# Four more tiles transposed by DMA, and a new order around them, in the opening of an FNet and MLP kernel

## The chip, the cores and the metric

The kernel runs on one core of one Trainium2 chip. The metric is the device time of one execution in microseconds (us), the median over runs of the same program. Besides the runs that are only timed there is one profiled execution, whose trace gives all durations below.

## The reference

The input is x of 2048 rows and 576 columns. It is normalized by row, and two branches are added to it: the real part of a Fourier transform over rows and columns, done with DFT matrices, and a two-layer MLP with a relu. All in float32.

```python
xn = (x - mean(x)) / sqrt(var(x) + 1e-5)            # by row, 2048 x 576
a = xn @ dft_hid_re.T;  b = xn @ dft_hid_im.T       # 576 x 576
y = dft_seq_re @ a - dft_seq_im @ b                 # 2048 x 2048
h = maximum(xn @ w1, 0)                             # w1: 576 x 4608
out = x + y + h @ w2                                # w2: 4608 x 576
```

## The kernel before

**Numbers.** Every float32 operand is split into two fp16 parts, hi and lo, and a product is three fp16 products (hi x lo, hi x hi, lo x hi), scaled by powers of two that the kernel computes from the data. Most products are done by a fast scheme of seven block products for a 2 x 2 blocking; hence the sums and differences on VectorE (DVE) around them.

**Tiling.** The 2048 rows are 16 tiles of 128 rows, tile t; four tiles are a group g of 512 rows (tiles 0 to 3 are group 0, and so on). The 4608 hidden columns are nine blocks b of 512. `xT[g]` holds the normalized rows of a group, transposed, in ten planes: nine with hi and lo, and a tenth with the last 128 hi columns again. A step is a pair (b, g), in the order of b, then g: `mlp1` multiplies a block of w1 by `xT[g]` into PSUM (four banks, `ps1`), `mlp1_out` applies the relu, splits the result and forms its sums (`h`), `mlp2` multiplies that by the split block of w2 (`w2s`) in seven products of 12 matmuls, into PSUM of the pool `ps2`, which has two buffers. The result is added into `acc`, and a DMA of GpSimd (POOL) with accumulation adds it to `spill[g, row, col]` in DRAM (L573). `spill` starts as a copy of x (L760), so that the residual is in it. The DFT branch follows after all steps, from about 815 us on.

**How a tile gets into xT.** `stats` computes mean and variance of several tiles on DVE, with one square root on ScalarE (ACT), and notes instructions in the dictionary `order`. `normalize` writes two things into the buffer `dbufs[t % 4]`: the float32 value (L247, DVE) and its fp16 hi part (L249, ACT). `remainder` forms the lo part (L253, L256; on POOL for tiles 1 to 11, on DVE for 0 and 12 to 15). Then comes one of two ways. `transposes` does ten transposes on TensorE (PE) into a PSUM buffer of `ps2` and copies them out with two ACT instructions (L279, L282); tiles 0 to 7 take it. `transposes_dma` issues two transposing DMAs from SyncE's queue (SP), a large one of nine planes (L265) and a small one of the tenth plane (L266); tiles 8 to 15 take it.

**The opening.** The steps (0, 0) and (0, 1) and half of the second product are written out by hand: group 0 is multiplied tile by tile as tiles arrive (`tile_by`, L324 with 128 columns), for group 1 the first two blocks of columns of w1 too, the other two as a whole (`q2`, 512 columns). Of block 0's weights, w1 comes first; for w2 a list `w` of steps is prepared (`prepare_w2`): two sums of absolute values on ACT (L646), then the scale (`power_pe`: a cast, L657, two small matmuls on PE, some small DVE operations, the last L669), then the splits (L182 on ACT, L183 on DVE) and sums (L678 to L681) which give `w2s`. After that a loop runs over the remaining steps; in step (0, 2) it normalizes and transposes tiles 12 to 15, and a list `todo` holds the work for block 1 (its loads, scales and splits), of which `work()` takes one item at a time.

**What sets the order.** The code's order is a priority. A planner with costs of its own places each engine's instructions: of those that it holds to be ready, the first in the code comes first. The result is fixed when the program is built, and every engine, and the queue of every engine that issues DMAs, runs its instructions in that order. `tc.issue_after(i)`, and `behind(key)` with an instruction noted in `order`, put what is traced inside behind `i`, but only those instructions which run on the same engine as `i`. Where an instruction reads or overwrites what another engine or a DMA has in use, it waits.

The calls around the change, today:

```python
copies of x: load_x(0..15), then 16 copies x -> spill        # all of them at the start, on SP
w[0](); w[1]()                                               # sums of w2, behind the root of tiles 4 to 7
N(4..7); E(4..7); T(4..7)                                    # through PE and ACT
weave(stats([8, 9, 10, 11], ("sh", 4)))
w[3]()                                                       # w2's scale, its cast behind ("sh", 8)
early = [mlp1(0, 2, 0), mlp1(0, 2, 1)]                       # behind three of mlp2's seven products
```

`N`, `E`, `T` and `TD` are short for `normalize`, `remainder`, `transposes` and `transposes_dma`.

## Time and profile before

| what | us |
|---|---|
| median of 3 runs | 1256.04 (1255.87 to 1256.17) |
| the profiled execution, its own time | 1256.51 |
| its span in the profile | 1254.7 |
| PE busy in the span | 1234.3 |
| DVE busy | 1008.9 |
| ACT busy | 704.8 |
| POOL busy | 155.6 |
| sixteen copies of x, first issue to last on SP | 18.07 to 30.84 |
| transposing DMAs of tiles 8 to 11 on SP | 39.66 to 52.04 |
| transposing DMAs of tiles 12 to 15 on SP | 72.55 to 86.14 |

PE is busy for 98% of the span, so what counts is where it is not, and what it waits for there. DVE has 80% over the whole span, but it is nearly full up to about 180 us. A row of the order of instructions gives start, duration, engine, line, operation, what it writes and reads, and how many such instructions follow one another; in brackets the idle time of the engine ahead of it and what ended that. "L" numbers are lines of the kernel before.

### The profile page before, as it was taken

Reading aid. Unit: us, or ns where it says so; the run is one execution under the profiler, and the core shown is the slowest. Engines: PE = TensorE matmul, PEld = TensorE weight load, DVE = VectorE, ACT = ScalarE, POOL = GpSimd, SP = SyncE. Lnnn points to the kernel's source line nnn. Section 1 sums busy time; section 2 is a strip of 40 time slices with the busy share of each in tenths; the row PEclk is TensorE's granted clock in tenths of the full one; section 3 lists DMA queues with packets and bytes.
Section 4 is the critical chain, followed back from the end, with each engine's and each line's share of the span. In section 5 each row is a group of like instructions: output and inputs, shape, how many; then the busy total and the mean of one; then the engine's idle time right before and its main releaser. Section 6 shows DMA issues by size and latency. Waiting matters only on the chain.

```text
span 1254.7 us, 25397 instructions
## 1 busy us (share of the span) xinstructions
PE 1234.3 (98%) x10309; PEld 983.5 (78%) x10309; DVE 1008.9 (80%) x1921; ACT 704.8 (56%) x1194; POOL 155.6 (12%) x199
## 2 busy tenths in 40 slices
PE   8799999999999999999999999999999999999998
PEld 7565657888888888888888888877777777777776
DVE  8999997878878778788787878566788878788885
ACT  5756566676666666766767666444453333333332
POOL 1321111212111111212121212100000000000000
PEclk9999999999999999999999999999999999999999
DMA  9576567666567665766576766630053434433420
GB/s 341 131 127 109 97 125 166 110 133 139 132 117 171 122 150 117 137 140 136 117 153 142 145 126 128 113 95 1 1 172 111 144 102 162 124 133 120 141 87 19
DMA packets 75909, 158.08 MB, mean 126 GB/s; under 512 B 17296, under 2 KB 36240, under 8 KB 75792
## 3 DMA queue, kind: packets, MB, share of 16 engines
q1 hardware_dynamic: 53008, 113.99, 28.3%
q0 software_dynamic: 22784, 42.48, 25.4%
q8 instruction: 80, 1.31, 0.4%
q14 instruction: 37, 0.30, 0.1%
HBM read 106.63 MB, written 51.90 MB: 126 GB/s over the span
## 4 chain that ended last, share of the span: by engine, by line
PE 74%; DVE 17%; DMA 4%; ACT 4%; issue 2%; POOL 0%; SPq 0%; DVEq 0%; ACTq 0%; POOLq 0%
PE p L1210 26%; PE p L556 19%; PE bank L479 19%; PE pd L1091 8%; DVE w2s L183 2%; DMA raw_w<-in_w_dram 1%; DMA acc<-in_x_dram 1%; DVE h L370 1%; PE p L324 1%; DVE h L501 1%; DVE h L377 1%; DMA f<-in_cre_dram 1%; ACT f L955 1%; DVE w1buf L183 1%; DVE dbuf L570 1%
## 5 line engine op out<-in xcount | busy, mean ns | idle before, releaser
L556 PE MATMUL p<-w2s,h 128*128 128x288 f16 x3024 | 409.8, 286 | 8.6 <-DVE w2s L183 3.3
L556 PEld LDWEIGHTS <-h 128*128 128x128 f16 x3024 | 295.5, 98 | 85.7 <-issue 9.8
L1210 PE MATMUL p<-R,cs 128*128 128x288 f16 x2688 | 329.4, 286 | 0.0
L1210 PEld LDWEIGHTS <-cs 128*128 128x128 f16 x2688 | 263.0, 98 | 66.3
L182 ACT ACTIVATE cs<-c,sc_c 128x1024 f16<-128x1024 f32 x112 | 125.1, 1144 | 196.8 <-DVE c L1153 72.6
L183 DVE SCALAR_TENSOR_TENSOR cs<-c,sc_c,cs 128x1024 f16<-128x1024 f32 x112 | 141.0, 1282 | 54.4 <-ACT cs L182 54.4
L479 PEld LDWEIGHTS <-w1buf 128*128 128x128 f16 x1600 | 156.5, 98 | 22.8 <-issue 1.7
L479 PEld LDWEIGHTS <-dbuf 128*128 128x128 f16 x1200 | 117.4, 98 | 17.5 <-issue 1.7
L479 PE MATMUL bank<-xT,w1buf 128*128 128x256 f16 x832 | 109.8, 273 | 0.0
L1091 PE MATMUL pd<-dbuf,xT 128*128 128x288 f16 x832 | 103.8, 286 | 0.0
L479 PE MATMUL bank<-acc,w1buf 128*128 128x256 f16 x768 | 102.1, 273 | 1.0 <-DVE acc L509 0.9
L1091 PEld LDWEIGHTS <-xT 128*128 128x128 f16 x832 | 80.8, 98 | 22.0 <-issue 1.9
L501 DVE TENSOR_TENSOR h<-s,h 128x1024 f16<-128x1024 f32 x56 | 68.5, 1223 | 33.9 <-ACT h L498 33.6
L573 POOL DMA_DIRECT2D spill<-dbuf x70 | 60.9, 875 | 233.1 <-DVE dbuf L570 201.9
L486 ACT ACTIVATE h<-acc 128x256 f16<-128x256 f32 x112 | 45.9, 411 | 77.5 <-DVE acc L509 74.8
L479 PE MATMUL bank<-xT,dbuf 128*128 128x256 f16 x624 | 82.4, 273 | 0.0
L498 ACT ACTIVATE h<-s 128x1024 f16<-128x1024 f32 x56 | 59.1, 1056 | 35.9 <-DVE s L493 35.1
L479 PE MATMUL bank<-acc,dbuf 128*128 128x256 f16 x576 | 76.6, 273 | 1.0 <-DVE acc L509 0.9
L1216 DVE SCALAR_TENSOR_TENSOR o<-p,us_c,o 128x288 f32<-128x288 f32 x112 | 57.5, 514 | 12.9 <-PE p L1210 12.3
L955 ACT ACTIVATE f<-f 128x1024 f32<-128x1024 f32 x64 | 66.9, 1046 | 0.6 <-DMA f<-in_cre_dram 0.6
L487 DVE SCALAR_TENSOR_TENSOR h<-acc,h 128x256 f16<-128x256 f32 x112 | 47.2, 422 | 21.0 <-ACT h L486 20.8
L573 POOL DMA_DIRECT2D spill<-sum x42 | 36.3, 865 | 184.9 <-DVE sum L570 159.8
(158 smaller groups left out, 1536.8 us busy)
## 6 DMA issues: line engine op xcount, KB each, us to landing
spill<-dbuf POOLq DMA_DIRECT2D x70, 288.0 KB, 5.2
f<-in_cre_dram SPq DMA_DIRECT2D x32, 512.0 KB, 5.8
f<-in_cim_dram SPq DMA_DIRECT2D x32, 512.0 KB, 5.2
c<-in_cre_dram SPq DMA_DIRECT2D x32, 512.0 KB, 4.1
c<-in_cim_dram SPq DMA_DIRECT2D x32, 512.0 KB, 5.0
spill<-sum POOLq DMA_DIRECT2D x42, 288.0 KB, 4.6
raw_w<-in_w_dram SPq DMA_DIRECT2D x17, 640.0 KB, 6.0
raw_w<-in_w_dram SPq DMA_DIRECT2D x18, 576.0 KB, 4.9
```

The source lines that it names most:

```text
L182: nc.scalar.activation(hi, src, AF.Copy, scale=s)
L183: nc.vector.scalar_tensor_tensor(lo, src, s, hi, ALU.mult, ALU.subtract)
L479: nc.tensor.matmul(ps, l, r, start=first and m == 0, stop=m == len(todo) - 1, skip_group_check=not first,)
L487: stt(lo, src, 0.0, hi, ALU.max, ALU.subtract)
L498: order["s"] = nc.scalar.activation(hi_s, st[:, 1:], AF.Copy).ins
L501: order["lo"] = nc.vector.tensor_tensor(lo_s, st[:, 1:], hi_s, ALU.subtract).ins
L556: order["pe"] = nc.tensor.matmul(ps[:, c], h[:, x, qa, c * P : (c + 1) * P], w[:, y, qb], start=first and i == 0 and j == 0, stop=i == NQ ...
L573: nc.gpsimd.dma_start(spill[g, row, col], o, accum_op=ALU.add)
L955: nc.scalar.activation(f, f, AF.Abs, scale=2.0**-10, accum_out=sums_c[:, n, q : q + 1])
L1091: nc.tensor.matmul(ps[j], xT[g][:, kx, c * P : (c + 1) * P], dsp[j][:, hl, k], start=(t % 2 == 0 and n == 0), stop=(t % 2 == 1 and n == le ...
L1210: nc.tensor.matmul(ps, w[:, a, k], r[:, c, rq], start=first and k == 0 and j == 0, stop=k == HK - 1 and j == 2, skip_group_check=not first,)
L1216: order["o"] = nc.vector.scalar_tensor_tensor(o, ps, us["c"][:, n : n + 1], o, ALU.mult, ALU.add).ins
```

## The change

- Tiles 4 to 7 go through `transposes_dma`. In it the small transpose now comes first, and each pair is put behind the pair before (`order["td"]`).
- The sixteen copies of x leave the start: four (group 0) are put behind tile 11's transposes, twelve behind tile 15's. The loads for the sums of the sequence DFT matrices (`first_c`) also come behind the last transposes.
- `transposes` is cut in two: `transposes` and `copies`. Tile 2's copies come behind the root of tiles 4 to 7.
- w2's cast comes behind the last aggregate of the statistics of tiles 8 to 11 (`order["stats"]`), and w2's scale in the code behind the first pair's outputs. `tile_by` of tiles 4 and 5 comes behind the scale's last small matmul (`order["pm"]`).
- Tiles 8 and 9 are normalized behind the first pair's DVE steps (`order["s4"]`). Tiles 10 and 11, and in the loop 12 to 15, have both parts of the normalization on ACT.
- In `mlp1_out` all DVE steps up to `s4` obey `after`; the second group's last pair gives `after="w2"`, the last of w2's splits.
- `early` is no longer put behind three of `mlp2`'s products; it stands ahead of all seven in the code.

```diff
@@ power_pe, split, stats
+        order["pm"] = nc.tensor.matmul(ps[:, 1, :n], ones, top, start=True, stop=True).ins
...
+            order["stats"] = nc.vector.bn_aggr(mv[:, i], st.rearrange("p a b -> p (a b)")).ins
@@ normalize
-        eng.tensor_scalar(xn, acc[t], means[t], factors[t], ALU.subtract, ALU.mult)
         with behind(after):
+            if eng is nc.scalar:
+                nc.scalar.activation(xn, acc[t], AF.Identity, bias=shifts[t], scale=factors[t])
+            else:
+                eng.tensor_scalar(xn, acc[t], means[t], factors[t], ALU.subtract, ALU.mult)
             nc.scalar.activation(xs[:, :D], acc[t], AF.Identity, bias=shifts[t], scale=factors[t])
@@ transposes_dma
-        nc.sync.dma_start_transpose(dst[:, :NKX], xs)
-        nc.sync.dma_start_transpose(dst[:, NKX], xs[:, D - P : D])
+        with behind("td"):
+            nc.sync.dma_start_transpose(dst[:, NKX], xs[:, D - P : D])
+            order["td"] = nc.sync.dma_start_transpose(dst[:, :NKX], xs).ins
@@ mlp1_out
             with behind(after):
-                nc.scalar.activation(hi, src, AF.Relu)
-            stt(lo, src, 0.0, hi, ALU.max, ALU.subtract)
-        stt(s3, a11, 0.0, r21, ALU.max, ALU.subtract)
...
+                order["hi"] = nc.scalar.activation(hi, src, AF.Relu).ins
+                stt(lo, src, 0.0, hi, ALU.max, ALU.subtract)
+        with behind(after):
+            stt(s3, a11, 0.0, r21, ALU.max, ALU.subtract)
...
+            order["s4"] = stt(s4, a12, 0.0, s2, ALU.max, ALU.subtract).ins
@@ power_w2, split_w2
-            with behind(("sh", 8)):
+            with behind("stats"):
                 nc.vector.tensor_copy(m, mx["w2", b])
...
-        with behind(None if b else ("xT", 7)):
-            split(w[:, 0, q], w[:, 1, q], src, sc["w2", b][:, i : i + 1])
+        with behind(None if b else "hi"):
+            order["w2"] = split(w[:, 0, q], w[:, 1, q], src, sc["w2", b][:, i : i + 1])
@@ the copies of x
-    for g, row, col in spill:
-        src = x[...]
-        nc.sync.dma_start(spill[g, row, col], src.rearrange("(c p) e -> p c e", p=P))
+    def copy_x(g):
+        for row, col in itertools.product(range(2), range(2)):
+            t = g * TG + row * 2
+            src = x[t * P : (t + 2) * P, col * EH : (col + 1) * EH]
+            with behind("td"):
+                nc.sync.dma_start(spill[g, row, col], src.rearrange("(c p) e -> p c e", p=P))
@@ the opening
-    T(2)
+    pt = transposes(2)
     split_w1(0, 3)
     N(3)
     E(3, GP)
     tile_by(0, (3,), ps)
     tile_by(1, (3,), ps)
+    weave(stats([4, 5, 6, 7]))
+    copies(2, pt, ("root", 4))
     T(3)
-    weave(stats([4, 5, 6, 7]))
-    N(4)
-    E(4, GP)
     w = prepare_w2(0)
     w[0]()
     w[1]()
     tile_by(2, (0, 1, 2, 3), ps)
-    for t in (5, 6, 7):
+    for t in (4, 5, 6, 7):
         N(t)
         E(t, GP)
-    T(4)
+        TD(t)
     tile_by(3, (0, 1, 2, 3), ps)
+    weave(stats([8, 9, 10, 11], ("sh", 4)))
     pq = ps2.tile([P, 2, 512], F32, tag="ps2", name="p1_0_1")
     qs = [pq[:, 0], pq[:, 1]]
...
     mlp1_out(0, 0, 0, *ps[:2])
+    w[3]()
+    with behind("pm"):
+        for t in (4, 5):
+            tile_by(t, (0, 1), qs)
+    for t in (8, 9):
+        N(t, after="s4")
+        E(t, GP)
+        TD(t)
+    mlp1_out(0, 0, 1, *ps[2:])
+    for t in (6, 7):
+        tile_by(t, (0, 1), qs)
+    for t in (10, 11):
+        N(t, nc.scalar, after="hi")
+        E(t, GP)
+        TD(t)
     w[4]()
+    w[6]()
+    mlp1_out(0, 1, 0, *qs)
+    q2 = [mlp1(0, 1, 2), mlp1(0, 1, 3)]
     w[5]()
+    for f in w[7:]:
         f()
+    mlp1_out(0, 1, 1, *q2, after="w2")
+    copy_x(0)
+    early = [mlp1(0, 2, 0), mlp1(0, 2, 1)]
+    for q in range(7):
         mlp2(0, 0, q)
@@ first_c
-        nc.sync.dma_start(f, blocks_c(n)[q])
+        with tc.issue_after(order["td"]):
+            nc.sync.dma_start(f, blocks_c(n)[q])
@@ the loop, step (0, 2)
-                normalize(t)
+                normalize(t, nc.scalar)
                 remainder(t, nc.vector)
                 transposes_dma(t)
...
         if n == 2:
+            for k in range(1, NG):
+                copy_x(k)
             for q in range(7):
                 mlp2(pb, pg, q)
```

59 lines of the change are left out of this document (16 added, 43 removed).

## Prediction, made before the changed kernel ran

> **What bounds the kernel now.** I read the page first, then the busy time in stretches of five microseconds, then the order of instructions up to 125 us, then the waits.
>
> ```profile
> PE 1234.3 (98%) x10309; PEld 983.5 (78%) x10309; DVE 1008.9 (80%) x1921; ACT 704.8 (56%) x1194; POOL 155.6 (12%) x199
> 30.00:35.00 5.00, 4.49 (x81) 4.49 (x82) 3.13 (x13) 5.00 (x12) 4.52 (x7) 1.00 1.06 303
> 45.00:50.00 5.00, 4.98 (x24) 2.18 (x23) 4.91 (x13) 2.66 (x5) 1.86 (x3) 1.00 0.99 186
> 50.00:55.00 5.00, 2.89 (x21) 1.83 (x20) 5.00 (x9) 3.57 (x6) 0.00 (x0) 1.00 0.35 66
> 55.00:60.00 5.00, 1.47 (x9) 0.71 (x8) 5.00 (x11) 2.64 (x4) 0.00 (x0) 1.00 0.28 76
> 60.00:65.00 5.00, 4.43 (x17) 2.08 (x16) 5.00 (x9) 1.69 (x2) 1.40 (x1) 0.66 0.67 196
> 80.00:85.00 5.00, 5.00 (x38) 3.55 (x37) 5.00 (x15) 2.06 (x3) 0.00 (x0) 1.00 1.37 180
> ```
>
> The columns after the window are its length, busy PE, PEld, DVE, ACT, POOL, the granted clock, the DMA share and GB/s. Over the span PE lacks 1254.7 - 1234.3 = 20.4 us, and 2.1 + 3.5 + 0.6 = 6.2 us of that lie between 50 and 65 us, the longest hole behind the start. DVE is full there: PE waits for VectorE's work on w2. From 65 us PE is full, so the kernel ends earlier by as much as PE reaches a fixed point of its work earlier, if nothing later gives it back. I take as that point the end of the second MLP product of the first group (84 matmuls at L556).
>
> ```profile
> 62.10 7.42 PE L324 MATMUL p<-xT,w1buf 128*128 128x512 f16 x28
> 69.36 6.04 PE L556 MATMUL p<-w2s,h 128*128 128x288 f16 x48
> 75.24 6.21 PE L324 MATMUL p<-xT,w1buf 128*128 128x512 f16 x28
> ```
>
> It lies at 69.36 + 6.04 = 75.4 us. What remains is paced by PE: 28 matmuls of 512 columns take 6.2 us (7.42 in the slow-clock stretch), and 84 at L556 take 84 x 6.04/48 = 10.6 us.
>
> **Part by part: the way to the transposed tiles.** Today tiles 4 to 7 are transposed on PE and copied out by ACT; tiles 8 to 11 go by DMA.
>
> ```profile
> 23.44 0.41 DVE L208 BATCH_NORM_AGGREGATE mv<-st 128x2 f32<-128x12 f32 x4
> 24.40 1.02 ACT L279 ACTIVATE xT<-pt 128x1024 f16<-128x1024 f16 x1 [1.28 <-PE pt L277]
> 25.32 0.38 ACT L282 ACTIVATE xT<-pt 128x256 f16<-128x256 f16 x1
> 25.58 0.30 ACT L215 ACTIVATE u<-mv,eps 128x4 f32<-128x4 f32 x1
> 28.08 0.88 ACT L249 ACTIVATE dbuf<-acc,sh,r 128x576 f16<-128x576 f32 x1
> 28.84 1.17 ACT L646 ACTIVATE w2s<-raw_w 128x1152 f16<-128x1152 f32 x1
> 29.90 0.21 ACT L646 ACTIVATION_READ_ACCUMULATOR w2s<-raw_w 128x1 f32 x1
> 31.20 1.16 POOL L256 TENSOR_TENSOR dbuf<-dbuf 128x512 f16<-128x512 f32 x1
> 32.31 0.31 POOL L253 TENSOR_TENSOR dbuf<-dbuf 128x64 f16<-128x64 f32 x1
> 42.45 1.28 SPq L265 DMA_TRANSPOSE xT<-dbuf  x1
> 50.81 1.23 SPq L266 DMA_TRANSPOSE xT<-dbuf  x1
> DMA to landing us min/median/max: 3.2/3.8/6.5
> ```
>
> The last row is of the large transposes (L265). The root of tiles 4 to 7 has its input at 23.85 and runs at 25.58, behind tile 2's copies. Put ahead of them it runs at 23.9: the statistics chain is 1.7 us earlier, and the copies still start at 24.4. On ACT two sums of w2 (1.17 + 0.21, 1.35 apart) and tile 3's copies (1.4) now come ahead of tile 4's normalization: 25.7 + 2 x 1.35 + 1.4 = 29.8, so its 0.88 ends at 30.7, against 28.96 now. ACT loses four pairs of copies after that (4 x 1.4 = 5.6 us). POOL's remainder takes 0.31 + 1.16, so tile 4's large transpose can be issued at 32.1. If ACT takes the tile ahead of the sums, this is 2.7 us earlier.
>
> Each tile needs a small and a large transpose, 1.23 + 1.28 us of SP's queue, near 2.6 with the gaps, and the DMA engines are 0.99 busy in 45 to 50 us, where they run. All sixteen are now in one strict order: tile 7's large one is issued at 32.1 + 3 x 2.6 = 39.9 and lands at 43.7; tile 11's at 32.1 + 7 x 2.6 = 50.3 and lands at 54.1. (The Trainium skill, "DMA: Bandwidth & Descriptors", section "Latency and other measured facts", gives DMA transposes 261 GB/s; by my estimate from it the 128 x 1280 x 2 bytes of a tile, 328 KB, would take 1.26 us, and tile 11's would be issued at 40.9 instead of 50.3. The trace's 2.6 us decides.) The large transposes now also keep their `dbuf` buffers, which the normalizations of tiles 8 to 11 write again, until they land.
>
> PE saves 40 transposes, but between tiles 4 and 7 it now waits for landings. A tile's 28 matmuls of group 1 take 1.75 us, hidden in the 2.6 us pace but for the last:
>
> ```profile
> 34.49 1.73 PE L324 MATMUL p<-xT,w1buf 128*128 128x128 f16 x28
> ```
>
> Tile 7 is done at 43.7 + 1.75 = 45.5, and the two following blocks of 28 end at 51.7. Then PE needs tiles 8 to 11 (54.1) for the two early blocks of group 2, or w2 for the second product. I let it wait for the tiles: 54.1 + 6.2 + 10.6 = 70.9 us, against 75.4. **Gain 4.5 us.** If two of the seven products fill 51.7 to 54.1 it is 6.9.
>
> **VectorE must keep up.** The same root also pulls its chain.
>
> ```profile
> 25.91 0.18 DVE L216 RECIPROCAL r<-u 128x4 f32<-128x4 f32 x1 [2.06 <-ACT u L215]
> 31.85 0.41 DVE L208 BATCH_NORM_AGGREGATE mv<-st 128x2 f32<-128x12 f32 x4
> 34.13 0.42 DVE L370 SCALAR_TENSOR_TENSOR h<-p,h 128x256 f16<-128x256 f32 x1 [1.87 <-ACT h L369]
> 40.48 1.13 DVE L657 CAST mb<-c_mw 128x2 bf16<-128x2 f32 x1
> 48.37 0.22 DVE L669 TENSOR_SCALAR c_sw<-c_pw,c_inv 128x2 f32<-128x2 f32 x1
> 58.86 1.01 DVE L370 SCALAR_TENSOR_TENSOR h<-p,h 128x256 f16<-128x256 f32 x2
> 59.80 0.81 DVE L183 SCALAR_TENSOR_TENSOR w2s<-raw_w,c_sw,w2s 128x576 f16<-128x576 f32 x1
> 64.06 1.23 DVE L377 TENSOR_TENSOR h<-s,h 128x1024 f16<-128x1024 f32 x1
> L247 DVE TENSOR_SCALAR dbuf<-acc,mv,r 128x576 f32<-128x576 f32 x4 | 2.1, 576 | 0.0
> ```
>
> From the aggregate's end (32.26) to w2's last split (60.6) lie 28.3 us of almost full DVE. Two normalizations leave it (tiles 10 and 11, 2 x 0.53 = 1.06), the last pair's first steps (1.01) move behind the splits, and the start is 1.7 earlier: 30.6 + 28.3 - 1.06 - 1.01 = 56.8. w2 is then ready 3.5 us before PE asks for it at 54.1 + 6.2 = 60.3; that is the cover, and past it each us costs one. The earlier scale (cast at about 31, not 40.48) adds no work: it only keeps the splits from waiting until 48.59. Its small operations now run beside POOL's remainders, where the cast took 1.13 us; five such instructions would eat 5 x 1 us at most, of which the 1.87 us that DVE idles ahead of 34.13 takes a part. The last pair's other steps end at 65.3 today (64.06 + 1.23) and are due when PE needs its banks again, at 70.9: covered. Tiles 12 to 15 take another 4 x 0.53 = 2.1 us off DVE.
>
> **The copies of x.** They leave 18 to 36 us, when nothing PE waits for is behind them. Four come behind tile 11 (about 52 to 56), and their accumulates come after 60. Twelve come behind tile 15, in front of the loads of block 1's w2 on SP.
>
> ```profile
> 18.07 12.77 SPq L760 DMA_DIRECT2D spill<-in_x_dram  x16
> 35.00:40.00 5.00, 4.67 (x82) 4.43 (x80) 4.86 (x15) 4.35 (x8) 0.41 (x2) 1.00 0.13 40
> 80.68 5.46 SPq L265 DMA_TRANSPOSE xT<-dbuf  x3
> 95.79 5.34 DMA raw_w<-in_w_dram
> 103.03 0.17 DVE L124 TENSOR_SCALAR half<-top 128x2 f32<-128x2 f32 x1 [0.82 <-POOL top L121]
> 139.95 3.10 PE L556 MATMUL p<-w2s,h 128*128 128x288 f16 x24
> ```
>
> SP took 0.80 us for each, and the DMA was busy until 35.6 (0.13 of the last five us), so a copy costs between 0.8 and 1.1 us (17.5 / 16). Tile 15's transposes end at 86.14, or 81.6 when shifted; twelve copies end at 91.2 to 94.8, and the second load of w2 lands 5.3 later, at 96.5 to 100.1. Shifted, it is due at 101.1 - 4.5 = 96.6. DVE, which already waited 0.82 us there, may so lose 0 to 3.5 us. PE first uses that w2 at 139.95, and only feels it through DVE's other work; I book nothing, and keep 3.5 as bound.
>
> The profiled run took 1256.5 us beside a span of 1254.7; the median before is 1256.04. Less 4.5 us: **1251.5 us** (profiled 1252.0). About 0.2%, 2.5 us, is what a measurement of this kernel can tell from no change.
>
> **Rivals.**
> *More gain (0.13).* The gap before 54.1 is filled, or tile 4 starts 2.7 us earlier: 6.9 to 7.2 us, about 1249. For it: seven products are ready by then in part. Against it: PE works in a fixed order.
>
> *A slow clock (0.10).* In 60 to 65 us PE got 0.66 of its clock after the hole, and 28 matmuls cost 7.42 instead of 6.21. Were PE, idle from about 32 to 35 and then paced by landings, to fall into that state, it costs 1.2 us or somewhat more: 1253. (The Trainium skill, "TensorE: Matmul & The Clock Gate", Part 1, says that about 3.4 us of idling halve the clock; the trace agrees, with 0.66 over five us.) Against it: the hole at 55 is what I expect to close.
>
> *The landings come late (0.15).* The landing row goes to 6.5 us where I took 3.8. With 2.7 more for tile 11 PE is at the fixed point at 73.6, a gain of 1.8: 1254.2. If ACT also puts the first pair's outputs ahead of the normalizations,
>
> ```profile
> 33.43 0.40 ACT L365 ACTIVATE s<-p 128x256 f32<-128x256 f32 x1
> 33.70 0.89 ACT L369 ACTIVATE h<-p 128x256 f16<-128x256 f32 x2
> ```
>
> 1.2 us more are lost: 1255.4. For it: one queue carries sixteen transposes without a pause. Against it: half of the eight large ones landed within 3.8. ACT's own new wait, for tile 7's buffer at 43.7, then two passes of 0.88 for tile 11, frees w2's splits at 45.5; DVE, by today's row, comes to them no earlier (48.59 - 1.7 - 1.06 = 45.8), so I give it no price.
>
> *Slower (0.20).* The twelve copies share the DMA with POOL's accumulates. At the 180 GB/s of 80 to 85 us a copy of 128 x 2 x 288 x 4 bytes, 295 KB, takes 1.64 us; they end at 81.6 + 19.7 = 101.3 and w2 lands at 106.6, 10.0 us late. DVE stands at the scale, everything behind it on DVE (the outputs of the first product, the adds of the second) stands too, and PE runs dry: 1251.5 + 10 = 1261.5. It decides from 1.18 us a copy, where the load lands as late as today. For it: that share of 1.37. Against it: PE holds several us of work that needs no DVE, and the old copies ran faster.
>
> **Numbers.** The forecast has 0.42, with a range of its own of 1249.5 to 1253.5 (the filled gap in part; 2 us of VectorE's bounds). Below 1253.5 lie the forecast, more gain and 0.7 of the slow clock: 0.62. Within 0.2%: the late landings and the rest of the slow clock, 0.18. Slower: 0.20. For eight in ten the range goes from 1247.5 to 1258.
>
> **What would show it.** Right: no L272 rows for tiles 4 to 7; sixteen transposes on SP at a pace near 2.6 us from about 31 to 51; c_sw (L669) near 36 instead of 48.37; w2's last split near 57; the clock at 1.00 in 60 to 65; the 84th matmul at L556 near 71. Wrong: transposes starting after 36, PE waiting for xT past 56, DVE idling around 100 at the scale of block 1, or PE stalls after 75 us that today are not there.

## The result and the profile after

The changed kernel took 1269.16 us (median of 4 runs, 1268.77 to 1270.53) against 1255.95 of the kernel before beside it: a ratio of 1.0107, 95% interval 1.0090 to 1.0125. It is slower by some 13 us; I had forecast 4.5 us faster. The profiled execution took 1268.89 us, with a span of 1267.1. Line numbers below are those of the changed kernel unless said otherwise: the matmul of the second product is L565 (L556 before), its evacuation on ACT L576, its addition on DVE L579, POOL's accumulate L582, the large and the small transposing DMA L270 and L269, a copy of x L774, the sum for w2's scale L655.

First PE, in order of time (start, duration, what it does, in brackets the idle time ahead and what ended it):

```profile
36.85 0.16 PE L166 MATMUL pm<-top,ones 1*128 1x2 bf16 x1 [5.23 <-DVE top L163]
54.39 6.20 PE L332 MATMUL p<-xT,w1buf 128*128 128x512 f16 x28 [2.36 <-ACT w2s L182]
66.15 6.31 PE L565 MATMUL p<-w2s,h 128*128 128x288 f16 x48 [1.15 <-DVE acc L579]
89.73 3.04 PE L565 MATMUL p<-w2s,h 128*128 128x288 f16 x12 [8.28 <-ACT acc L576]
98.97 3.10 PE L565 MATMUL p<-w2s,h 128*128 128x288 f16 x24
120.57 2.68 PE L565 MATMUL p<-w2s,h 128*128 128x288 f16 x12 [2.17 <-ACT acc L576]
127.99 2.97 PE L332 MATMUL p<-xT,dbuf 128*128 128x512 f16 x13
```

And the same places of the kernel before that are not shown yet:

```profile
81.28 10.74 PE L556 MATMUL p<-w2s,h 128*128 128x288 f16 x84
114.05 2.97 PE L324 MATMUL p<-xT,dbuf 128*128 128x512 f16 x13
```

The prediction's fixed point, the end of the 84th matmul, lies at 66.15 + 6.31 = 72.46 us, 2.9 earlier than before. (The row at 54.39 puts the wait down to a split on ACT that ended at 54.27; tile 11's transpose, which these matmuls read, landed at 54.2, so either can have ended it.) Then PE loses the gain and more. Group 1's products are through after the 168th matmul of the second product: at 98.97 + 3.10 = 102.07 us, with three matmuls of step (0, 3), 0.8 us, ahead of its last 24; in the kernel before at 81.28 + 10.74 = 92.02. The first matmul of step (1, 0) starts at 127.99 us, 114.05 before. So 102.07 - 0.8 - 92.02 = 9.3 us, and with the 2.9 that were ahead 12.2, are lost between 72 and 102, and 13.9 - 9.3 = 4.6 more up to 128.

Busy time in stretches of five microseconds (columns as in the prediction) shows the two places, and the clock behind them:

```profile
80.00:85.00 5.00, 1.45 (x12) 1.01 (x11) 4.33 (x11) 3.06 (x6) 0.00 (x0) 1.00 1.19 149
85.00:90.00 5.00, 0.27 (x2) 0.18 (x2) 1.66 (x2) 1.78 (x3) 0.00 (x0) 0.68 1.35 153
90.00:95.00 5.00, 4.17 (x19) 2.44 (x18) 4.17 (x7) 1.88 (x3) 0.00 (x0) 0.50 0.79 192
95.00:100.00 5.00, 5.00 (x31) 3.32 (x30) 1.44 (x3) 1.26 (x2) 1.09 (x1) 0.79 1.00 325
115.00:120.00 5.00, 3.00 (x19) 1.66 (x18) 3.18 (x14) 2.89 (x6) 0.36 (x1) 1.00 0.16 28
120.00:125.00 5.00, 4.43 (x18) 2.39 (x18) 4.69 (x7) 3.91 (x7) 0.00 (x0) 0.66 0.01 3
```

In 80 to 90 us PE works 1.7 of 10 us, and then runs at half its clock; at 115 it starves again. What ACT, DVE, POOL and SP do around these places, and how long group 3's large transposes take from issue to landing (last row):

```profile
62.69 1.54 DVE L115 TENSOR_REDUCE c_mf<-raw_w 128x1 f32<-128x640 f32 x2 [2.82 <-DMA raw_w<-in_w_dram]
88.22 0.83 ACT L182 ACTIVATE dbuf<-raw_w,c_sw 128x640 f16<-128x640 f32 x1 [5.16 <-DMA xT<-dbuf]
114.35 1.16 ACT L655 ACTIVATE j<-raw_w 128x1152 f32<-128x1152 f32 x1 [5.02 <-DMA raw_w<-in_w_dram]
116.18 0.17 DVE L124 TENSOR_SCALAR half<-top 128x2 f32<-128x2 f32 x1 [4.80 <-POOL top L121]
50.89 1.32 SPq L270 DMA_TRANSPOSE xT<-dbuf  x1
52.26 2.65 SPq L774 DMA_DIRECT2D spill<-in_x_dram  x4
75.02 3.53 POOL L582 DMA_DIRECT2D spill<-acc  x3
77.08 2.85 SPq L270 DMA_TRANSPOSE xT<-dbuf  x1
92.64 7.69 SPq L774 DMA_DIRECT2D spill<-in_x_dram  x11
105.43 0.34 SPq L100 DMA_DIRECT2D raw_w<-in_w_dram  x1
DMA to landing us min/median/max: 3.4/5.2/11.1
```

*First place.* Block 1's first w1 split on ACT (88.22) writes the buffer `dbuf` that tile 12's transpose still reads; that transpose was issued at 77.08, beside three accumulates of POOL (75.02), and landed 11.1 us later. Behind the split in ACT's queue stands the evacuation for which PE waits 8.28 us. *Second place.* The sum over block 1's second w2 load (114.35) waits for its landing; the load was issued at 105.43, behind eleven copies of x, where the kernel before had issued it at 95.8. The scale (116.18) waits for the sum.

So there were two suspects. **Theory W** (the wait): the split stands in ACT's queue ahead of the evacuations, and group 3's transposes come too late for it. **Theory C** (the copies): the copies of x behind the transposes hold up what follows them on the DMA queue.

### The profile page after: what moved, and what is told of

Its sections match the earlier page's. It is cut to its first block, busy times and chain, and to the rows that moved or that the text cites. A ratio compares the mean times of both kernels' runs of the same rounds, so it can differ in the third digit from the quotient of the medians.

```text
span 1267.1 us, 25321 instructions
## 1 busy us (share of the span) xinstructions
PE 1234.7 (97%) x10269; PEld 984.6 (78%) x10269; DVE 1008.2 (80%) x1915; ACT 704.5 (56%) x1192; POOL 156.6 (12%) x199
## 4 chain that ended last, share of the span: by engine, by line
PE 79%; DVE 13%; ACT 3%; DMA 3%; issue 2%; POOL 0%; SPq 0%; ACTq 0%; DVEq 0%; POOLq 0%
PE p L1225 26%; PE p L565 22%; PE bank L488 21%; PE pd L1106 8%; PE p L332 2%; DMA raw_w<-in_w_dram 2%; DVE w2s L183 1%; DMA xT<-dbuf 1%; DVE h L386 1%; DVE h L378 1%; ACT w2s L182 1%; DVE w1buf L183 1%; DVE h L510 1%; DVE c_mf L115 0%; DVE sum L579 0%
## 5 line engine op out<-in xcount | busy, mean ns | idle before, releaser
L565 PE MATMUL p<-w2s,h 128*128 128x288 f16 x3024 | 412.5, 288 | 14.6 <-ACT acc L576 11.7
L565 PEld LDWEIGHTS <-h 128*128 128x128 f16 x3024 | 297.2, 98 | 92.8 <-issue 16.1
L582 POOL DMA_DIRECT2D spill<-dbuf x70 | 61.0, 876 | 233.5 <-DVE dbuf L579 201.7
L576 ACT ACTIVATE dbuf<-p,c_ub 128x576 f32<-128x576 f32 x70 | 51.1, 731 | 16.0 <-PE p L565 15.7
```

Of the source, the lines that this page charges most:

```text
L565: order["pe"] = nc.tensor.matmul(ps[:, c], h[:, x, qa, c * P : (c + 1) * P], w[:, y, qb], start=first and i == 0 and j == 0, stop=i == NQ ...
L576: freed(nc.scalar.activation(o, ps, AF.Copy, scale=us[b]))
L582: nc.gpsimd.dma_start(spill[g, row, col], o, accum_op=ALU.add)
```

## The experiments

All runs in one table: the median, the ratio to the kernel before beside it with its 95% interval, and from the profiled execution the start of the first matmul of step (1, 0).

| run | us | ratio | interval | (1, 0) starts at |
|---|---|---|---|---|
| before | 1256.04 | 1 | | 114.05 |
| changed | 1269.16 | 1.0107 | 1.0090 to 1.0125 | 127.99 |
| a1_copies_start | 1264.97 | 1.0067 | 1.0048 to 1.0086 | 122.48 |
| a2_split_late | 1266.09 | 1.0074 | 1.0059 to 1.0089 | 127.12 |
| a3_no_acc | 1266.85 | 1.0082 | 1.0067 to 1.0097 | 123.74 |
| a4_before_copies | 1265.87 | 1.0074 | 1.0059 to 1.0089 | 124.26 |
| c1_copies_split | 1263.16 | 1.0060 | 1.0043 to 1.0078 | 121.08 |
| c2_stats_first | 1268.36 | 1.0097 | 1.0082 to 1.0112 | 126.83 |
| c3_both | 1260.77 | 1.0036 | 1.0023 to 1.0050 | 119.46 |
| b1_dve_norm | 1269.47 | 1.0103 | 1.0086 to 1.0120 | 128.63 |
| d1_stats_ahead | 1257.05 | 1.0001 | 0.9992 to 1.0010 | 115.49 |
| d5_tiles45_pe | 1257.83 | 1.0009 | 1.0000 to 1.0019 | 119.07 |
| d6_all_pe | 1267.81 | 1.0094 | 1.0078 to 1.0111 | 124.66 |
| e1_before_split | 1256.51 | 1.0002 | 0.9992 to 1.0011 | 114.71 |
| f1_products_first | 1252.42 | 0.9969 | 0.9957 to 0.9981 | 110.75 |
| f2_fill | 1255.81 | 1.0000 | 0.9989 to 1.0011 | 112.82 |
| f3_d1_products_first | 1256.36 | 1.0005 | 0.9997 to 1.0014 | 113.37 |
| h1_before_products | 1257.58 | 1.0005 | 0.9996 to 1.0015 | 115.49 |
| h2_late_copies | 1265.77 | 1.0064 | 1.0049 to 1.0079 | 126.19 |
| h3_stats_as_changed | 1258.05 | 1.0005 | 0.9996 to 1.0015 | 116.44 |

From that start to the end of the span lie 1137.7 to 1141.2 us in every row. So what differs is decided, but for 3.5 us, in the first tenth of the run.

### One cause at a time, first attempt

**a1_copies_start.** The changed kernel, all sixteen copies at the start again.

```diff
+    for k in range(NG):
+        copy_x(k)                # right behind the loads of x
-    copy_x(0)                    # behind tile 11's transposes
-            for k in range(1, NG):
-                copy_x(k)        # behind tile 15's
```

> The changed kernel with all sixteen copies of x issued at the start again, as in the kernel before; everything else of the change stays. Theory C (the copies behind the transposes cost the time: four of them stand ahead of block 1's w1 loads, so that the statistics of tiles 12 to 15 start 2.8 us late, and eleven stand ahead of block 1's second w2 load, which lands at 114.3 us where it landed at 95.8): the w1 loads are issued near 52 us, the w2 load lands near 96, both losses go, and the time is 1252 to 1257 us. Theory W (block 1's first w1 split stands on ScalarE and VectorE ahead of product evacuations and waits there for tile 12's transpose): the second loss of 7.5 us goes, the PE stall of some 8 us near 82 to 90 us stays, and the time is 1260 to 1263 us. The price: the copies fill the DMA engines until about 35 us, so the transposes of tiles 4 to 7 may land later, and the 84th matmul of the first 512-column product group's second set end at 74 to 76 us instead of 72.5.

1264.97 us: between the two. (The 95.8 us in this and the fourth expectation, with which the load of the kernel before is said to land, is its issue; it landed at 101.1. The second loss, 7.5 us in the texts, was counted across matmuls that the planner had moved; it is 4.6.) PE's two long waits, and ACT's fp16 parts of tiles 8 to 11:

```profile
59.32 7.93 PE L332 MATMUL p<-xT,w1buf 128*128 128x512 f16 x28 [6.88 <-DMA xT<-dbuf]
92.46 1.02 PE L332 MATMUL p<-xT,w1buf 128*128 128x512 f16 x4 [3.67 <-DMA xT<-dbuf]
44.67 3.13 ACT L252 ACTIVATE dbuf<-acc,sh,r 128x576 f16<-128x576 f32 x4
```

The second loss is gone, and so is the long wait near 89; but the price at the front was higher than expected: 6.88 us of waiting for tile 11, and the 84th matmul at 77.5 us instead of 72.46. Tile 11's large transpose was issued at 55.83 us instead of 50.89. The copies, which fill the DMA engines up to 35 us (a share of 1.05), can account for at most 2.0 us of that: tile 7's was issued at 41.27 instead of 39.30. The rest came with ACT's planned order, which has the fp16 parts of tiles 8 to 11 all together at 44.67; in the change the first starts at 35.64. So this run changed more than the place of the copies.

**a2_split_late.** Block 1's w1 splits behind the second group's evacuations.

```diff
-                for _ in range(6):
+                for _ in range(6 if i < 3 else 0):
                     work()
...
+        with behind("free" if b == 1 else None):
             split(w[:, 0, k], w[:, 1, k], raws["w1", b, i][:, k], ...)
```

> The changed kernel with block 1's first w1 splits placed behind the last evacuation of block 0's second product group, so that no evacuation is queued behind a split that waits for tile 12's transpose; the copies stay where the change put them. Theory W: the PE stall of 8.3 us that ends at 89.7 us goes, and the granted clock of 0.50 from 87 to 97 us with it; the first product after it starts 8 to 10 us earlier than at 98.2 us; 1259 to 1261 us. Theory C: the stall has another end, the time stays at 1267 to 1270 us. Both theories leave the second loss, near 116 to 125 us, in place, unless the later split runs into block 1's start itself.

1266.09 us. The wait of 8.28 us on ACT went as theory W said, but PE met three others:

```profile
83.66 1.63 PE L565 MATMUL p<-w2s,h 128*128 128x288 f16 x12 [1.57 <-ACT acc L576]
95.53 3.01 PE L565 MATMUL p<-w2s,h 128*128 128x288 f16 x12 [5.14 <-DVE acc L579]
119.94 3.04 PE L565 MATMUL p<-w2s,h 128*128 128x288 f16 x12 [4.69 <-ACT acc L576]
```

The later split frees its buffer later, and block 1's w2 loads, which go into the same buffers, were issued at 107.4 and 122.3 us. Moving the waiting instruction moved the wait.

**a3_no_acc.** The accumulates of block 0's first group left out.

```diff
-        if n not in (0, 2, 3):
+        if n not in (0, 2, 3) and (b or g):
             nc.gpsimd.dma_start(spill[g, row, col], o, accum_op=ALU.add)
```

> The changed kernel without the accumulates that GpSimd sends to DRAM for block 0's first group; that contribution is left out of the output, and so are their 3.5 us of descriptor work each and their bytes. If tile 12's large transpose takes 11.1 us because it shares the DMA engines with those accumulates, it lands in 4 to 5 us, the split is released at about 82 us, the PE stall shrinks from 8.3 to at most 2 us, and the time is 1260 to 1263 us. If the transpose is late for another reason (its own queue, the late start alone), the stall stays at 6 us or more and the time at 1266 to 1269 us.

Group 3's large transposes now all landed in 3.2 to 3.4 us, and the wait on ACT shrank to 3.10:

```profile
DMA to landing us min/median/max: 3.2/3.3/3.4
85.10 2.62 PE L565 MATMUL p<-w2s,h 128*128 128x288 f16 x12 [3.10 <-ACT acc L576]
```

So the 11.1 us of tile 12 were the accumulates beside it: shown. (The 3.5 us in the expectation are those of three accumulates together, the row at 75.02.) But the time fell only to 1266.85 us, since the second loss stayed (ACT then waited 7.12 us for the w2 load).

**a4_before_copies.** The kernel before, with the copies alone moved to where the change has them.

```diff
-    for g, row, col in spill: ...                   # the sixteen copies at the start
+    copy_x(0)                                       # behind TD(11)
...
+            for k in range(1, NG): copy_x(k)        # behind tile 15's transposes
```

> The kernel before with one part of the change alone: the copies of x moved from the start to behind the transposes, four behind tile 11's and twelve behind tile 15's. Theory C: the w1 loads of block 1 are late and its second w2 load lands 10 to 18 us later than at 95.8 us, VectorE and ScalarE stand at that split: 1259 to 1265 us. If the copies are harmless in the old order: 1255 to 1257 us. Theory W has no term here unless tile 12's transpose becomes late too.

1265.87 us, ratio 1.0074 (1.0059 to 1.0089): with every other part of the change away, the place of the copies costs 9 us, at the sum that waits for block 1's second w2 load (L646 in this kernel) and at PE behind it:

```profile
112.69 1.16 ACT L646 ACTIVATE j<-raw_w 128x1152 f32<-128x1152 f32 x1 [11.50 <-DMA raw_w<-in_w_dram]
115.11 4.44 PE L556 MATMUL p<-w2s,h 128*128 128x288 f16 x24 [8.50 <-ACT acc L567]
```

Each cure left most of the loss standing: the two causes cover each other. In the changed kernel the second w2 load would have been late for either: the copies were issued by 100.33 us, and then the load waited 5.0 more for the split to free its buffer.

### Both causes

**c1_copies_split.** Copies in two holes of the DMA engines.

```diff
+    copy_x(0); copy_x(1)                            # at the start
-    copy_x(0)                                       # behind TD(11)
-            for k in range(1, NG): copy_x(k)        # behind tile 15's transposes
-            [lambda: (load_w1(b, 0), load_w1(b, 1))] + wait
+            [lambda: (load_w1(b, 0), load_w1(b, 1), b == 1 and (copy_x(2, "lw"), copy_x(3, "lw")))] + wait
```

> The changed kernel with the copies of x in two holes of the DMA engines: the eight of groups 0 and 1 at the start, the eight of groups 2 and 3 right behind block 1's w1 loads; nothing else of the change is touched. Theory C and W together (both late copies and the split's wait cost time): the second loss goes (block 1's second w2 load lands at 96 to 104 us where it landed at 114), block 1's w1 data land 1 to 2 us earlier, but the accumulates still share the DMA engines with tile 12's transposes, so a PE stall of 5 to 8 us before 90 us stays: 1258 to 1262 us. Theory C alone: 1252 to 1255 us. Theory W alone (the second loss is only the consequence of the split's lateness, since the load waited 5.0 us for the split that frees its buffer): 1265 to 1269 us.

1263.16 us. The second loss went; PE's wait of 8.48 us for ACT's evacuation, ending at 89.08, stayed.

**c2_stats_first.** One order on DVE.

```diff
-        with behind("vfree" if b >= BB else ("sh", 1) if f > 1 else None):
+        with behind("vfree" if b >= BB else "stats" if b == 1 else ("sh", 1) if f > 1 else None):
             magnitude(...)                          # the maxima of w1
```

> The changed kernel with one order added: VectorE takes block 1's w1 maxima behind the statistics of tiles 12 to 15, not ahead of them. It then has no 2.8 us wait for those loads ahead of the statistics, so tile 12's transposes are issued at 71 to 73 us instead of 75.9; ScalarE's first block 1 split falls behind two evacuations of block 0's second product group. Theory W: the PE stall of 8.3 us goes to under 2 us and the time is 1258 to 1262 us, with the second loss left. Theory C: the stall before 90 us is halved at most and the copies still hold block 1's second w2 load until 112 us or later: 1264 to 1268 us.

1268.36 us. The wait of 8.3 us went, but not by the way I had said: tile 12's transposes were issued later, not earlier (78.0 us). Two other things helped: the planner set the split behind two evacuations, and the large transposes, now behind the accumulates of 72.7 and 74.2 us, landed within 4.5 us. PE then lost 7.44 us at 117.31 us to the copies.

**c3_both.** The edits of c1 and c2 together.

> Both edits together: copies of x in the two holes, and statistics of tiles 12 to 15 ahead of block 1's w1 maxima. If the two losses are these two causes and nothing else, neither is left, and the 2.9 us won at the front show: 1251 to 1254 us, below the kernel before. If a third cause stands behind them (the transposes of tiles 12 to 15 at the pace of 2.7 us a tile against the accumulates), 1256 to 1262 us.

1260.77 us: the larger number. The third cause stood in DVE's queue. In it the first product's addition comes ahead of the statistics of tiles 12 to 15, and since the change puts the blocks of `early` ahead of all products, DVE waits for PE there:

```profile
66.26 0.82 DVE L579 SCALAR_TENSOR_TENSOR acc<-p,c_ub,acc 128x576 f32<-128x576 f32 x1 [3.40 <-PE p L565]
67.00 2.96 DVE L205 BATCH_NORM_STATS2 st<-acc 128x6 f32<-128x288 f32 x8
77.36 1.14 SPq L269 DMA_TRANSPOSE xT<-dbuf  x1
92.69 0.38 PE L332 MATMUL p<-xT,w1buf 128*128 128x512 f16 x1 [3.26 <-DMA xT<-dbuf]
```

**b1_dve_norm.** The change's ACT normalization of tiles 12 to 15 undone.

```diff
-                normalize(t, nc.scalar)
+                normalize(t)
```

> The changed kernel with the float32 normalization of tiles 12 to 15 on VectorE again, as in the kernel before; copies and orders stay. Each of the four took 0.61 us on VectorE and 0.85 us on ScalarE. ScalarE then reaches the first block 1 split with four instructions less ahead of it, and the planned order puts that split behind two evacuations. Theory W: the stall of 8.3 us shrinks to under 3 us: 1260 to 1264 us. Theory C: 1266 to 1269 us.

1269.47 us, no gain: PE lost 3.83 us at 92.11 us for tile 15 and 8.55 at 118.71 us behind the late w2 load instead. A miss for the numbers of theory W, and one more case of the second loss showing as soon as the first is gone.

**d1_stats_ahead.** c3, and the statistics of tiles 12 to 15 placed in the code ahead of block 0's first products.

```diff
+    with tc.issue_after(order["lo"]):
+        weave(stats([12, 13, 14, 15]))
     for q in range(7):
         mlp2(0, 0, q)
```

> The run with both edits (copies of x in two holes, w1 maxima behind the statistics), and the statistics of tiles 12 to 15 planned ahead of block 0's first products. With both edits alone, VectorE stood 3.40 us at the first product's addition for a matmul, with those statistics queued behind it, and tile 12's transposes were issued at 77.4 us; PE then waited 3.26 us for tile 15's at 92.7 us. If the order of VectorE's queue is what keeps group 3's transposes late, they are issued at 71 to 73 us, the wait at 92.7 us goes with its clock dip (0.87 and 0.79 from 90 to 100 us), and the time falls by 3 to 5 us to 1255 to 1258 us. If group 3's transposes are late by the DMA engines' sharing with the accumulates, the wait stays at 2 to 4 us and the time at 1259 to 1261 us.

1257.05 us, 1.0001: the loss is gone. Tile 12's transposes start at 74.52 us (later than I said), PE's wait for tile 15 falls to 1.55 us, and no dip of the clock follows.

**e1_before_split.** The kernel before with the copies of c1.

> The kernel before with the copies of x in the two holes: eight at the start, eight behind block 1's w1 loads; no other edit. Theory C says that the place of the copies alone costs the 9 us that the kernel before loses with all copies late; here none stands ahead of a w2 load, so 1254 to 1258 us. If it is the copies' traffic at any place behind 55 us that costs, 1259 us or more.

1256.51 us: the copies are harmless in those two places. It is what stands behind them on the queue that counts.

### Where the front's gain went

**d6_all_pe.** The changed kernel with tiles 4 to 7 transposed on PE.

```diff
     for t in (4, 5, 6, 7):
         N(t)
         E(t, GP)
-        TD(t)
     tile_by(3, (0, 1, 2, 3), ps)
+    for t in (4, 5, 6, 7):
+        T(t)
```

> The changed kernel with tiles 4 to 7 transposed by PE, as in the kernel before, everything else of the change kept, the late copies too. If the DMA transposes of tiles 4 to 7 are worth the 2.9 us at the 84th matmul of the first second-set product, this loses 2 to 4 us at the front and keeps the second loss: 1268 to 1273 us. If the loss comes from the later stages alone and the front matters little, 1264 to 1270 us.

1267.81 us (1.0094, 1.0078 to 1.0111), against 1.0107 (1.0090 to 1.0125) of the change: no difference that these runs can tell. The front is as early as with all eight by DMA:

```profile
61.82 10.45 PE L565 MATMUL p<-w2s,h 128*128 128x288 f16 x84
```

The 84th matmul ends at 72.27 us, where the change has 72.46 and the kernel before 75.4. So the transposes by DMA, the first part of the change, are worth nothing here, and the gain at the front is there without them, from the rest of the change; which part of that gives it was not run.

**d5_tiles45_pe.** d1, with only tiles 4 and 5 on PE, in its 5.23 us hole before the broadcast.

```diff
-        TD(t)
+        if t > 5:
+            TD(t)
     tile_by(3, (0, 1, 2, 3), ps)
+    T(4)
+    T(5)
```

> The same, with tiles 4 and 5 transposed by PE, in the 5.2 us that PE waits there for its broadcast, and only 6 to 11 by DMA. If the pace of eight transposes on one queue (2.65 us a tile from 29.2 us on) is what eats the front's gain, tile 11 lands some 5 us earlier, PE's 3.0 us wait for it at 55 us goes with the clock of 0.66 behind it, and the time is 2 to 4 us below the run without this edit: 1252 to 1255 us. If w2's splits end the front anyway, 1255 to 1258 us.

1257.83 us, no gain; but in the profiled execution (1259.73 us) PE stood, after 144 matmuls of the second product, at a first matmul of step (0, 3) that the planner had set ahead of the last 24 of group 1:

```profile
91.08 0.61 PE L332 MATMUL p<-xT,w1buf 128*128 128x512 f16 x1 [5.77 <-DMA xT<-dbuf]
90.00:95.00 5.00, 3.92 (x16) 2.41 (x17) 0.39 (x1) 0.00 (x0) 0.00 (x0) 0.52 0.94 274
```

It was there at 85.3 us. The kernel before passed that point at 92.02 less 24 matmuls, 3.1 us: at 88.9. The front was 3.6 us ahead (the 6.5 in the next expectation forgets the 24 matmuls), and the wait with its clock of 0.52 gave it all back.

**f1_products_first.** The same, with two products of group 2 ahead of that matmul.

```diff
+            elif n == 3 and i == 0:
+                for q in range(2):
+                    mlp2(pb, pg, q)
+                with tc.issue_after(order["pe"]):
+                    mlp1_step(b, g, i, ps)
...
-                mlp2(pb, pg, q)
+                if n > 3 or i:
+                    mlp2(pb, pg, q)
```

> The run with tiles 4 and 5 on PE, and PE's order in block 0's fourth group changed: two products of the third group ahead of the first fourth-group matmul, which needs tile 15's transpose. In the run before it PE was ready at 85.3 us, 6.5 us earlier than in the kernel before (91.86 us), stood 5.77 us for tile 15 and ran at 0.52 and 0.80 of its clock from 90 to 100 us. If the front's gain of this change is real and is handed back at that wait alone, the wait shrinks to under 1.5 us and the time falls 4 to 7 us below that run: 1250.5 to 1253.5 us, below the kernel before. If VectorE's and ScalarE's work between there and block 1 is the bound (the gain is an order of PE's queue, not less work), PE meets other waits of the same sum by 125 us: 1255 to 1258 us.

1252.42 us, ratio 0.9969 (0.9957 to 0.9981): faster than the kernel before by some 3.4 us. Step (0, 3) starts at 91.53 us with two more products done, (1, 0) at 110.75, 3.3 earlier than before. PE's waits between 40 and 180 us that are longer than half a microsecond are these two:

```profile
52.69 6.22 PE L332 MATMUL p<-xT,w1buf 128*128 128x512 f16 x28 [1.25 <-DMA xT<-dbuf]
80.23 1.63 PE L565 MATMUL p<-w2s,h 128*128 128x288 f16 x12 [1.76 <-ACT acc L576]
```

**f2_fill.** f1 with idle work in the hole before the broadcast, to hold the clock up.

```diff
+        if n == 2:
+            for _ in range(18):
+                nc.tensor.matmul(ps[:, 1, 256:], xT[0][:, 0, :P], xT[0][:, 0, :256], start=True, stop=True)
...
+    with behind("pm"):
+        q2 = [mlp1(0, 1, 2), mlp1(0, 1, 3)]
```

> The same, with 18 matmuls of no use (128x256, into the unused half of the broadcast's bank) in the 2.43 us hole before the broadcast at 37.5 us, and the second group's last pair of blocks kept behind the broadcast. If that hole is what takes the granted clock to 0.56 and 0.76 from 35 to 45 us, and PE is the bound behind it, the clock is 1.0 there and the time 2 to 3 us below the run without it. If the earlier hole of 1.60 us, or the landings of tiles 6 to 11, set the stage, no change.

1255.81 us, slower than f1. The clock was 1.00 in all stretches from 30 to 130 us, where f1 has 0.82 and 0.84 from 35 to 45, but the broadcast came at 39.03 us instead of 37.25 (the planned order of DVE around it had changed too).

```profile
39.12 18.72 PE L337 MATMUL p<-xT,w1buf 128*128 128x128 f16 x168
62.96 1.63 PE L570 MATMUL p<-w2s,h 128*128 128x288 f16 x12 [2.18 <-ACT acc L581]
```

PE was all the same through the early blocks at 57.8 us, 1.1 earlier than in f1 (58.9), and lost that again right behind, in a wait of 2.18 us that f1 does not have there. So the run does not settle what the dip costs.

**f3_d1_products_first.** f1's order of PE with all eight tiles by DMA.

> The kernel with copies in two holes and the statistics ahead (1257.05 us, all eight tiles by DMA), with only the order of PE's queue changed as above. There the wait for tile 15 was 1.55 us: 1255 to 1257 us. If the eight DMA transposes cost nothing against six, as good as the run with tiles 4 and 5 on PE; if their chain holds the front, 2 to 4 us above it.

1256.36 us: 1.0005 (0.9997 to 1.0014) against f1's 0.9969, some 4 us more. PE waited 5.24 us for the broadcast at 37.28 and for tile 11 before the early blocks:

```profile
55.44 6.20 PE L332 MATMUL p<-xT,w1buf 128*128 128x512 f16 x28 [2.81 <-DMA xT<-dbuf]
```

Tile 11's large transpose was issued at 51.94 us, 2.5 later than in f1 (49.42), and step (1, 0) starts 2.6 later. So eight tiles on one queue instead of six bring a later tile 11, and with it 2.6 us; the two profiled executions differ by 2.7 us in all (1254.49 and 1251.80).

**h1_before_products.** The kernel before with that order of PE.

> The kernel before with only PE's order of the best run: two products of the third group ahead of the fourth group's first matmul. The kernel before shows no wait there (first fourth-group matmul at 91.86 us, no idle ahead of it), so 1255 to 1258 us. If it comes out at 1253 us or less, the best run's gain is this order and not the front of the change.

1257.58 us, no gain: the order alone does not give f1's gain, which needs the new front.

**h2_late_copies.** f1, with the copies where the change has them.

> The best run (1252.42 us) with the copies of x put back to where the change has them, four behind tile 11's transposes and twelve behind tile 15's; statistics, tiles 4 and 5 on PE and PE's order as in it. This is the copies' price with nothing else late. Theory C: block 1's second w2 load is issued behind eleven copies, lands at 108 us or later, PE stands 6 to 9 us near 110 us with a clock dip behind it, 1260 to 1264 us. If the copies cost only in company with the split's wait, 1252 to 1255 us.

1265.77 us; by the two ratios (1.0064 and 0.9969) 12 us more than f1. The price of the copies with nothing else late, on SP, ACT and PE, and of block 1's two w2 loads from issue to landing:

```profile
91.99 6.34 SPq L774 DMA_DIRECT2D spill<-in_x_dram  x7
98.38 0.67 SPq L966 DMA_DIRECT2D f<-in_cre_dram  x1
100.00 2.63 SPq L100 DMA_DIRECT2D raw_w<-in_w_dram  x1
DMA to landing us min/median/max: 6.9/10.8/14.7
114.74 1.16 ACT L655 ACTIVATE j<-raw_w 128x1152 f32<-128x1152 f32 x1 [13.35 <-DMA raw_w<-in_w_dram]
116.67 5.40 PE L565 MATMUL p<-w2s,h 128*128 128x288 f16 x24 [10.17 <-ACT acc L576]
105.00:110.00 5.00, 1.50 (x7) 0.58 (x6) 0.00 (x0) 0.00 (x0) 0.00 (x0) 1.00 1.17 246
110.00:115.00 5.00, 0.00 (x0) 0.00 (x0) 0.00 (x0) 0.26 (x1) 0.00 (x0) 0.62 0.67 257
```

ACT and DVE stand still from 105 us on, the DMA engines are full up to 110 us (1.17, then 0.67), and PE has 1.5 us of work in ten. (2.8 of the 15.4 us by which step (1, 0) is later than in f1 lie ahead of step (0, 3): the planned order of the front had changed too. The row at 98.38 is a load of 512 KB for the sums of the DFT matrices, which stands ahead of the w2 load as well.)

**h3_stats_as_changed.** f1, with statistics and maxima in the order of the change.

> The best run with the statistics of tiles 12 to 15 and block 1's w1 maxima ordered as in the change (the statistics planned behind block 0's first products). This is the price of that order with the copies out of the way. Theory W: tile 12's transposes are issued 2 to 3 us later than at 73 us, the first block 1 split or PE's fourth group waits for group 3's transposes: 1255 to 1260 us. If the order costs nothing once PE has other products to do: 1252 to 1254 us.

1258.05 us; by the ratios (1.0005 and 0.9969) 4.5 us more than f1. Here the split does not wait for a DMA; ACT's queue just has the late normalizations of tiles 12 to 15 and the split ahead of the evacuation that PE needs:

```profile
80.70 1.54 ACT L182 ACTIVATE dbuf<-raw_w,c_sw 128x640 f16<-128x640 f32 x2
84.27 0.72 ACT L576 ACTIVATE acc<-p,c_ub 128x576 f32<-128x576 f32 x1
85.05 7.42 PE L565 MATMUL p<-w2s,h 128*128 128x288 f16 x48 [6.52 <-ACT acc L576]
```

## Why the prediction was wrong

**The front was nearly right.** Tile 4's large transpose was issued at 31.19 us (predicted 32.1), tile 11's at 50.89 (50.3) and landed 3.3 us later, at 54.2 (54.1); w2's last split ended at 57.48 (56.8); PE began the early blocks at 54.39 (54.1). The fixed point came at 72.46 instead of 70.9, and the term that was mis-sized is the 1.15 us that PE stood before the last 48 matmuls: DVE's addition was queued behind a maximum that waited 2.82 us for block 1's w1 load. PE's idling before 36.85 was not for landings but 5.23 us for the broadcast, and it did bring the clock down, to 0.56 and 0.75 from 35 to 45 us, as the rival of the slow clock said; PE was through with the tiles by 52.0 all the same (51.7 predicted). w2's scale came at 43.1, not near 36, and no split that PE waited for was late by it. But the sum takes the gain from the way of the tiles into xT, and with tiles 4 to 7 back on PE the fixed point is as early (72.27 us). That the time of the front came out near the forecast is thus in part luck: the gain is there without the transposes that the sum went through.

**The step that failed: the copies.** I priced a copy at 0.8 to 1.1 us and let the load land at 96.5 to 100.1 us. In the changed kernel it landed at 105.43 + 8.8 = 114.2, held by the split too, and in the run with nothing else late at 100.0 + 14.7 = 114.7. Three terms were off. The twelve copies start at 88.07 us there, not at 81.6. Ahead of the load stand also block 1's first w2 load, as large as two copies of 288 KB, and the DFT load of 512 KB; the sum had neither. And each 288 KB took 1.35 us in the mean, beside accumulates: from 88.07 to 114.7, less 5.3 us for the load alone, are 21.3 us for 15.8 times 288 KB. (In the kernel before with only the copies moved, without the DFT load, it is 1.45: from 87.06 to 97.60 + 15.0, less 5.3, for 14 times.) That is beyond the 1.18 us from which the rival of a slower kernel decides. That rival was the right mechanism; I gave it 0.20, and 10 us.

The worse error is why I booked nothing: "PE first uses that w2 at 139.95, and only feels it through DVE's other work", and against the rival, "PE holds several us of work that needs no DVE". The wait for the load does not strike where PE reads w2. It strikes at the sum on ACT and the scale on DVE, and behind these in the same two queues stand the evacuations and additions of all products. PE, with two buffers for the products, was dry within some microseconds (10.17 us of wait in that run, 8.50 in the kernel before with only the copies moved).

**The step that was missing: group 3.** "Tile 15's transposes end at 86.14, or 81.6 when shifted" took it that the loop shifts with the front. Its statistics stand in DVE's queue behind a load and an addition that do not shift, so tile 12's large transpose was issued at 77.08 us, 2 us later than before, into the accumulates of group 0. The prediction looked at ACT's wait for the buffer of tile 7, not at the same wait of block 1's first split for tile 12's buffer. Each piece has its run: without the accumulates the landing falls from 11.1 to 3.4 us; with the statistics in the changed order and the copies out of the way 4.5 us are lost; with both causes away the loss is gone (1.0001).

**"If nothing later gives it back."** This condition failed a third time: with both losses removed the gain of the front was handed back at PE's own order, at the wait for tile 15. Only with that changed, and with tiles 4 and 5 back on PE, it shows, as 3.4 us of the 4.5 forecast. So most of the forecast gain is there in a kernel, but not in this change, and not with all four tiles moved to the DMA.

Of the signs listed as "wrong", two came: DVE idle at block 1's scale (4.80 us, at 116), and PE stalls after 75 us. Transposes after 36 us and PE waiting for xT past 56 did not.

**Open.** What the stretch of slow clock from 35 to 45 us costs was not settled, since the filled hole delayed the broadcast and came with another order behind it. Whether the best run would keep its gain with all four tiles on PE was not run. That tile 12's landing alone decides the wait of the first place was shown only in part: with fast landings 3.10 us of it remained, from the order of ACT's queue. The order in which the planner sets instructions also moved with each edit (in the run with the late copies by 2.8 us at the front), so the prices of 12 and 4.5 us hold to about 3 us.

## What to carry to other kernels

Price a late load by what is queued behind the first instruction that waits for it, on that instruction's engine, and not by when its data is finally multiplied. Before a transfer is moved to a quieter-looking place, list what is issued behind it on its queue and with whom it will share the engines: the same sixteen copies cost nothing in two holes and 9 to 12 us in front of one load. When one cure of a loss brings little, apply the next one on top of it before giving up either: here two causes hid each other, and the gain showed only with both away, PE's order adapted and two of the tiles back on PE. And undo the part of a change that its forecast rests on, by itself: here the front stayed as early without it.

## What the runs showed of the hardware

A transposing DMA of nine planes that lands in 3.2 to 3.4 us with POOL's accumulates left out took up to 11.1 us beside three of them (6.5 in the kernel before, tile 12).

Short holes can bring PE's clock down. In the run with the statistics ahead 2.39 us of waiting was followed by 0.66 of the clock from 55 to 60 us, and 1.96 us in the run with the split copies by 0.69; after 8.28 us in the changed kernel it was 0.68, 0.50 and 0.79 over three stretches of five. But 1.25 and 1.76 us in the best run left it at 1.00, and so did 2.36 us in the changed kernel (at 54.39) and 2.81 us in f3 (at 55.44). So by these rows the length of a hole near 2 us does not decide by itself; what else does was not found. (The Trainium skill, "TensorE: Matmul & The Clock Gate", Part 1, puts the switch to half the clock behind an idle window of about 3.4 us; by these rows a hole of 2 us can be enough. The 0.66 of the kernel before, with which the prediction says the trace agrees, stands behind several holes of at most 1.87 us each.)
